# Reordering the first loads and the first attention units of an attention-plus-MLP kernel

## The chip, the cores and the metric

The kernel runs on one core of a Trainium2 chip. Its engines have in-order instruction queues and meet through semaphores: TensorE (matmuls and transposes, into PSUM), VectorE, ScalarE (activations and copies), GpSimd (here it issues nearly all loads, and makes some copies and masks), and SyncE (it issues stores and transposing DMAs). The metric is device time in microseconds of one launch. The kernel before takes 286.05 us in the median of three runs (285.69 to 287.41).

## What is computed

The inputs are q, k and v of shape (8, 8, 576, 64): batch, heads, sequence, head size. Attention goes over a window of 32 positions to either side; its result, reshaped to 4608 tokens of 512 features, goes through a two-layer network with weights w_in (512 x 2048) and w_out (2048 x 512):

```python
scores = scale * np.matmul(q, k.transpose(0, 1, 3, 2))
mask = np.abs(pos[:, None] - pos[None, :]) <= window
attn = np.exp(scores) / sum                  # after the mask, max subtracted
x = (attn @ v).transpose(0, 2, 1, 3).reshape(4608, 512)
h = x @ w_in
out = (h * sigmoid(1.702 * h)) @ w_out
```

## The kernel before

The 4608 tokens are 36 units of 128 queries; four units make a tile of 512 tokens. Since one sequence has 576 tokens, unit 4 is the first that straddles two sequences. For one unit, `scores(u)` (L248) makes the scores of eight heads in two PSUM banks and ScalarE's exponentials of them; `band(u)` (L268) multiplies by the mask on VectorE; `values(u)` (L276) multiplies by the values on TensorE, with a column of ones that gives the sum; `norm(u)` (L294) divides on VectorE. Each unit needs the values of its own 128 keys (`ve`) and the same values shifted by 64 (`vo`), which `odd_v(u)` (L208) copies in two halves: half 1 from unit u, half 0 from unit u + 1. `x_T` and `x_T2` (L308, L323) transpose one or two units of the attention's result for layer 1.

Layer 1 of tile 0 runs in 16 blocks, `layer1_plain(0, d, half, tag)` (L388): eight matmuls of 256 columns for 256 hidden features (d) and half of the tile's tokens, into the PSUM bank `tag`, then the activation on ScalarE (L400). Later tiles use a scheme with seven products in place of eight (`l1_group`, L417), which needs sums of the weights (`w1_sums`, L337). Layer 2 of tile 0 is a list of 64 matmuls of 512 columns (`layer2_plain`, L474), from which `do(self.l2, n)` takes the next n; the first 8 need the first quarter of w_out, the next 8 the second, and so on.

PSUM banks have names: t (two banks), A, C, B, E, LA, LB. A new use of a bank waits until its last reader is done. `keep_busy(n, tag, cols)` (L563) issues n dummy matmuls into a bank.

The order of the work is the order in which it is written: each engine's queue takes its instructions in program order. The opening (`opening`, L572 to L712) is written out by hand, and brings the kernel from the first loads to the start of tile 1's layer 1. It transposes the queries and keys of units 0 to 3 by TensorE in two parts (`load_first` L137, `T_first` L157), and those of tile 1 in one (`load_four` L173, `T_four` L181). Loads of one kind: `load_w1(c)` (L113) brings the c-th quarter of w_in, `load_w2(c)` (L118) that of w_out, `load_v(u)` (L194) the values of one unit, in two DMAs if the unit straddles two sequences, `load_v_part(lo, n)` (L201) those of n tokens. All of these are issued by GpSimd, between its other work: the mask (`setup_mask` L99; `cut_mask` L108, which clears the corners for units that straddle sequences) and some of the `odd_v` copies.

```python
for b, rows, cols in ((0, hi, slice(0, 32)), (0, lo, slice(32, 64)), (2, lo, slice(0, 32)), (2, hi, slice(32, 64))):
    self.nc.gpsimd.memset(self.mask[rows, b, cols], 0.0)
```

`band` reads blocks 1 and 3 of the mask for a unit inside one sequence, and block 0 or 2 for one that straddles two.

## Time and profile before

| | us |
|---|---|
| median of three runs | 286.05 |
| the profiled execution | 285.67 |
| its span | 284.0 |
| TensorE busy | 275.8 (97%) |
| VectorE busy | 215.7 (76%) |
| ScalarE busy | 193.6 (68%) |
| GpSimd busy | 131.3 (46%) |
| end of the opening on TensorE | 46.2 |

All places in time are microseconds from the start of the span. PE is TensorE's matmuls, PEld its weight loads, DVE VectorE, ACT ScalarE, POOL GpSimd, SP SyncE. A row of a timeline gives start, length, engine, line, operation, what is written and read, and in square brackets the idle time before it with what ended that time. A row of DMA issues gives the count, the size at the destination and the time from issue to landing. A line L70 is the helper through which all matmuls go, and L67 that of copies, so names of tiles tell them apart: h is layer 1, o layer 2, sc scores, pv values, tp transposes, kq and kst, qst keys and queries.

### The profile page before, as it was taken

The page shows a single profiled execution, that of the slowest core. Times are in us where ns is not written, and L with a number is a line of the kernel's source. Part 1 is how long each engine was busy: PE and PEld are TensorE (multiplying, and loading weights), DVE is VectorE, ACT ScalarE, POOL GpSimd, SP SyncE. Part 2 cuts the span into 40 slices and gives each one's busy share as a digit, 9 for nine tenths or more (in the row PEclk, how much of TensorE's full clock was granted, in tenths as well). Part 3 has the DMA queues.
Part 4 walks back from the last instruction along what each step waited for, and adds up shares of the span by engine and source line. Part 5 has one row for each costly group of instructions (what it writes and reads, how often), then busy time and mean ns, then how long its engine had stood idle before and what let it go on. Part 6 is the DMA issues. An engine that isn't in the chain of part 4 may idle for free.

```text
span 284.0 us, 9223 instructions
## 1 busy us (share of the span) xinstructions
PE 275.8 (97%) x3819; PEld 229.7 (81%) x3819; DVE 215.7 (76%) x496; ACT 193.6 (68%) x340; POOL 131.3 (46%) x199
## 2 busy tenths in 40 slices
PE   7999999999999999999999999999999999999994
PEld 7677857776777888888888788888888888888883
DVE  1758796897988888797878787888788878945631
ACT  2556775889797769667966796588758775567410
POOL 8967487896699871847084809331110000000000
PEclk9999999999999999999999999999999999999999
DMA  8999999999999999999999999994423031201033
GB/s 93 188 193 198 185 202 158 197 134 141 181 142 164 182 126 203 136 180 149 172 128 189 120 180 112 188 119 107 132 56 96 2 111 21 76 0 74 2 112 115
DMA packets 147003, 37.38 MB, mean 132 GB/s; under 512 B 133904, under 2 KB 142608, under 8 KB 146960
## 3 DMA queue, kind: packets, MB, share of 16 engines
q0 software_dynamic: 104480, 18.42, 95.5%
q1 hardware_dynamic: 42032, 17.84, 32.3%
q8 instruction: 30, 0.49, 0.7%
q10 hardware_dynamic: 448, 0.52, 0.6%
q14 instruction: 13, 0.11, 0.1%
HBM read 36.83 MB, written 9.44 MB: 163 GB/s over the span
## 4 chain that ended last, share of the span: by engine, by line
PE 80%; DMA 8%; POOL 4%; ACT 2%; DVE 2%; issue 1%; POOLq 0%
PE o L70 37%; PE h L70 36%; DMA w<-in_moe_w_out_dram 4%; DMA o_sb<-in_k_dram 4%; PE pv L70 3%; PE sc L70 2%; POOL ve L199 2%; ACT p L266 1%; POOL kq L143 1%; PE tp L332 1%; POOL w L115 1%; PE tp L242 1%; DVE x L304 1%; ACT g L429 1%; DVE h L442 0%
## 5 line engine op out<-in xcount | busy, mean ns | idle before, releaser
L429 ACT ACTIVATE g<-h 128x512 f16<-128x512 f32 x128 | 72.2, 598 | 36.1 <-PE h L70 35.9
L70 PEld LDWEIGHTS <-g 128*128 128x128 f16 x576 | 54.4, 98 | 9.7
L70 PEld LDWEIGHTS <-a 128*128 128x128 f16 x512 | 49.2, 97 | 11.4 <-issue 1.2
L70 PE MATMUL h<-xs,a 128*128 128x256 f16 x384 | 57.6, 273 | 0.4 <-DVE h L442 0.2
L70 PE MATMUL o<-w,g 128*128 128x256 f16 (+1 forms) x320 | 55.3, 295 | 0.1
L70 PEld LDWEIGHTS <-w 128*128 128x128 f16 x512 | 48.8, 98 | 7.0 <-DMA w<-in_moe_w_in_dram 0.3
L70 PE MATMUL h<-xT,w 128*128 128x256 f16 x384 | 54.1, 273 | 0.2 <-DMA w<-in_moe_w_in_dram 0.2
L199 POOL DMA_DIRECT2D ve<-in_v_dram x39 | 33.3, 859 | 36.3 <-issue 34.2
L70 PEld LDWEIGHTS <-gs 128*128 128x128 f16 x384 | 36.7, 98 | 5.2 <-issue 0.4
L266 ACT ACTIVATE p<-sc 128x512 bf16<-128x512 f32 x72 | 36.6, 621 | 3.3 <-PE sc L70 3.3
L70 PE MATMUL o<-b,gs 128*128 128x256 f16 x256 | 37.7, 273 | 0.5 <-ACT o L67 0.5
L70 PE MATMUL o<-b,g 128*128 128x256 f16 x256 | 37.3, 273 | 0.0
L442 DVE TENSOR_TENSOR h<-h,s 128x512 f32<-128x512 f32 x32 | 22.3, 698 | 18.9 <-PE h L70 18.9
L67 ACT COPY h<-h 128x512 f32<-128x512 f32 x32 | 18.9, 589 | 15.9 <-PE h L70 15.5
L304 DVE TENSOR_TENSOR x<-pv,rec 128x256 f16<-128x256 f32 (+1 forms) x53 | 27.6, 520 | 1.8
L131 POOL DMA_DIRECT2D kst<-in_k_dram x31 | 26.5, 856 | 5.3 <-DMA w<-in_moe_w_out_dram 2.2
L131 POOL DMA_DIRECT2D qst<-in_q_dram x35 | 28.0, 804 | 1.8 <-DMA qT<-qst 1.2
L274 DVE TENSOR_TENSOR p<-p,mask 128x1024 bf16<-128x1024 bf16 x36 | 24.8, 691 | 4.9 <-ACT p L266 4.3
L218 POOL COPY vo<-ve 64x264 int32<-64x264 int32 x31 | 15.5, 500 | 26.2 <-PE pv L70 24.8
L448 DVE TENSOR_TENSOR h<-h,s 128x512 f32<-128x512 f32 x32 | 22.4, 699 | 4.7 <-PE h L70 4.2
L67 ACT COPY s<-h 128x512 f32<-128x512 f32 x32 | 19.2, 601 | 1.3
L70 PE MATMUL h<-xs,w 128*128 128x256 f16 x128 | 19.2, 273 | 0.0
(86 smaller groups left out, 367.9 us busy)
## 6 DMA issues: line engine op xcount, KB each, us to landing
out_dram<-o_sb SPq DMA_DIRECT2D x33, 256.0 KB, 3.2
ve<-in_v_dram POOLq DMA_DIRECT2D x31, 128.0 KB, 6.0
kst<-in_k_dram POOLq DMA_DIRECT2D x25, 128.0 KB, 6.4
qst<-in_q_dram POOLq DMA_DIRECT2D x21, 128.0 KB, 6.0
w<-in_moe_w_in_dram POOLq DMA_DIRECT2D x4, 512.0 KB, 8.7
w<-in_moe_w_out_dram POOLq DMA_DIRECT2D x4, 512.0 KB, 11.9
qst<-in_q_dram POOLq DMA_DIRECT2D x7, 96.0 KB, 5.4
ve<-in_v_dram POOLq DMA_DIRECT2D x10, 64.0 KB, 7.8
```

Of the source, the lines that this page charges most:

```text
L67: (eng.copy if eng is self.nc.scalar else eng.tensor_copy)(out, in_)
L70: self.nc.tensor.matmul(out, lhsT, rhs, start=start, stop=stop, skip_group_check=True)
L115: self.nc.gpsimd.dma_start(self.w1[:, :, c * 512:c * 512 + w], self.w_in[:, c * 512:c * 512 + w].rearrange("(k p) f -> p k f", p=128))
L131: self.nc.gpsimd.dma_start(t[off:off + n], src[b, :, s:s + n, :].rearrange("h s d -> s h d"))
L199: self.nc.gpsimd.dma_start(t[off:off + n, :, :self.D], self.v[b, :, s:s + n, :].rearrange("h s d -> s h d"))
L218: eng.tensor_copy(words(vo[64:128]), words(self.ve[u % 9][64:128]))
L266: self.nc.scalar.activation(p[:, eo].rearrange("k h s -> k (h s)"), sc[eo], AF.Exp, scale=self.scale)
L274: (eng or self.nc.vector).tensor_mul(pv, pv, msk.to_broadcast([128, 8, 2, SQ]))
L304: dve.tensor_mul(x[:, 4 * at:4 * (at + n), :].rearrange("p (b h) d -> p b h d", b=n), acc[:, :, :, :D], r.to_broadcast([128, n, 4, D]))
L429: act.activation(g[:, f, 256 * half:256 * half + 256], bank.rearrange("p (i n) -> p i n", i=2), AF.Gelu_apprx_sigmoid)
L442: dve.tensor_add(e, b, s7)
L448: dve.tensor_add(c, b, s7)
```

## The change

Only `opening` changes. Among the loads, the second keys and queries of units 0 to 3 go ahead of the first quarter of w_in; the values of unit 3 and the first half of unit 4's go ahead of its second quarter, and the other half behind its fourth; `odd_v(3)` on GpSimd moves up behind tile 1's keys; `cut_mask` moves down to where `odd_v(6)` is issued, which on GpSimd's queue is behind the keys of unit 8. The memset of `idle` is cut into eight.

Units 2 and 3 are then transposed and scored directly behind units 0 and 1, with other banks and copying engines; the layer-1 blocks of tile 0 follow in the order (half 0: d 0 to 3), (half 1: 0 to 3), (half 0: 4, 5), (half 1: 4, 5), (half 0: 6, 7), (half 1: 6, 7), where before it was half 0: 0 to 5, half 1: 0 to 5, half 0: 6, 7, half 1: 6, 7. From unit 4 on, the layer-2 matmuls stand in other places, 20 of them instead of 24 within the opening; those left over run later, at the next `do(self.l2)` without a count (L819).

```diff
-        dve.memset(self.idle, 0.0)
+        for i in range(8):
+            dve.memset(self.idle[:, 64 * i:64 * i + 64], 0.0)
...
         for u in (0, 1, 2):
             self.load_v(u)
+        self.load_first("k", 1)
+        self.load_first("q", 1)
         self.load_w1(0)
         self.setup_mask()
-        self.load_first("k", 1)
-        self.load_first("q", 1)
-        self.cut_mask()
+        self.load_v(3)
+        self.load_v_part(512, 64)
         self.load_w1(1)
-        self.load_v(3)
-        self.load_v(4)
         self.load_w1(2)
         self.load_four("k")
+        self.odd_v(3, pool)
         self.load_four("q")
         self.load_w1(3)
-        self.odd_v(3, pool)
+        self.load_v_part(576, 64)
...
         self.norm(0)
         self.norm(1)
-        self.keep_busy(2, "E")
-        self.x_T(0, "LA", act)
-        self.keep_busy(4, "E")
-        self.x_T(1, "LB", act)
-        self.T_first("k", 1, "AC", (dve, dve))
...
-        self.layer1_plain(0, 0, 0, "B", gelus)
-        self.T_first("q", 1, ("LA", "LB"), (dve, act))
-        self.layer1_plain(0, 1, 0, "E", gelus)
-        h[:] = ["B", "E", "LB", "LA", "B", "E", "LB", "LA"]
+        self.T_first("k", 1, "BE", (act, act))
+        self.T_first("q", 1, ("LA", "LB"), (act, dve))
+        self.x_T(0, "B", dve)
+        self.x_T(1, "E", dve)
         self.odd_v(2, dve, (1,))
+        self.keep_busy(3, "LA")
         self.scores(2, "t")
         self.scores(3, "AC")
-        self.layer1_plain(0, 2, 0, "LA", gelus)
-        self.layer1_plain(0, 3, 0, "LB", gelus)
-        self.do(gelus)
...
+        l1(0, 0, "B")
+        l1(0, 1, "E")
         self.band(2)
         self.odd_v(2, dve, (0,))
         self.band(3)
-        self.keep_busy(4, "t")
         self.values(2, "t")
         self.norm(2)
-        self.keep_busy(4, "A")
+        self.keep_busy(3, "LA")
         self.values(3, "AC")
         self.norm(3)
-        l1(0, 4)
+        self.keep_busy(8, "LA")
+        l1(0, 2, "LA")
         self.x_T2(2, "A", dve)
-        l1(0, 5)
+        l1(0, 3, "LB")
...
         for i in (3, 1, 2):
             self.w1_sums((i,), 0)
+        self.cut_mask()
         for u in (6, 7):
             self.odd_v(u, pool)
...
-        l1(1, 0, 1)
+        l1(1, 0, "B")
+        l1(1, 1, "E")
+        l1(1, 2, "LA")
+        l1(1, 3, "LB")
         self.T_four("k", "AC", (dve, dve))
...
-        l1(1, 2, 3)
+        l1(0, 4, "B")
+        l1(0, 5, "E")
         self.T_four("q", "AC", (dve, act))
-        l1(1, 4, 5)
+        l1(1, 4, "LB")
+        l1(1, 5, "LA")
+        for i in (3, 1):
+            self.w1_sums((i,), 1)
         self.odd_v(4, dve)
+        self.odd_v(5, dve, (1,))
         self.scores(4, "t")
         self.scores(5, "AC")
-        for i in (3, 1):
-            self.w1_sums((i,), 1)
         for d, tag in ((6, "B"), (7, "E")):
             self.layer1_plain(0, d, 0, tag, gelus)
-        self.do(self.l2, 3)
         self.scores(6, "t")
-        self.do(self.l2, 3)
+        self.do(self.l2, 4)
         self.scores(7, "AC")
         self.do(gelus)
-        self.do(self.l2, 2)
+        self.do(self.l2, 4)
         self.band(4)
-        self.odd_v(5, dve)
         self.band(5)
         self.band(6)
+        self.odd_v(5, dve, (0,))
         self.values(4, "t")
...
         self.band(7)
-        self.do(self.l2, 4)
         self.values(6, "t")
         self.norm(6)
-        self.do(self.l2, 4)
+        l1(1, 6, "B")
         self.values(7, "AC")
         self.norm(7)
-        l1(1, 6, 7)
+        l1(1, 7, "E")
+        self.do(self.l2, 4)
         self.x_T2(4, "A", act)
         self.do(self.l2, 4)
         self.x_T2(6, "t", dve)
         self.do(self.l2, 4)
```

More of the change, by code (lines that the diff above doesn't have):

```diff
@@ L627, in opening, with l1 @@
         self.norm(1)
-        self.keep_busy(2, "E")
-        self.x_T(0, "LA", act)
-        self.keep_busy(4, "E")
-        self.x_T(1, "LB", act)
-        self.T_first("k", 1, "AC", (dve, dve))
-        h, n, gelus = [], [0], []
-        def l1(half, *ds):
-            for d in ds:
-                self.layer1_plain(0, d, half, h[n[0] % len(h)])
-                n[0] += 1
-        self.layer1_plain(0, 0, 0, "B", gelus)
-        self.T_first("q", 1, ("LA", "LB"), (dve, act))
-        self.layer1_plain(0, 1, 0, "E", gelus)
-        h[:] = ["B", "E", "LB", "LA", "B", "E", "LB", "LA"]
+        self.T_first("k", 1, "BE", (act, act))
+        self.T_first("q", 1, ("LA", "LB"), (act, dve))
+        self.x_T(0, "B", dve)
+        self.x_T(1, "E", dve)
         self.odd_v(2, dve, (1,))
+        self.keep_busy(3, "LA")
         self.scores(2, "t")
         self.scores(3, "AC")
-        self.layer1_plain(0, 2, 0, "LA", gelus)
-        self.layer1_plain(0, 3, 0, "LB", gelus)
-        self.do(gelus)
+        gelus = []
+        def l1(half, d, tag):
+            self.layer1_plain(0, d, half, tag)
+        l1(0, 0, "B")
+        l1(0, 1, "E")
         self.band(2)
@@ L699, in opening @@
         self.band(7)
-        self.do(self.l2, 4)
         self.values(6, "t")
         self.norm(6)
-        self.do(self.l2, 4)
+        l1(1, 6, "B")
         self.values(7, "AC")
         self.norm(7)
-        h[:] = "BE"
-        n[0] = 0
-        l1(1, 6, 7)
+        l1(1, 7, "E")
+        self.do(self.l2, 4)
         self.x_T2(4, "A", act)
```

## The prediction

> **What bounds the kernel now.** I read the page first (engine shares, the chain that ended last), then the chain in order of time, then each engine's timeline over the first 90 us, then the landing times of single DMAs.

> ```profile
> span 284.0 us, 9223 instructions
> PE 80%; DMA 8%; POOL 4%; ACT 2%; DVE 2%; issue 1%; POOLq 0%
> ```

> TensorE holds 80% of the chain. The profiled run took 285.67 us, so 1.67 us lie around the span of 284.0; the median of the three runs, 286.05, is 0.38 above that run, and I add my difference to the median.

> ```profile
> 88.00:284.00 196.00, 191.76 (x2443) 165.62 (x2441) 150.88 (x350) 131.66 (x235) 61.33 (x94) 1.00 1.10 116
> 46.23:66.00 19.77, 19.75 (x168) 14.71 (x167) 17.52 (x34) 15.76 (x30) 18.71 (x27) 1.00 2.03 163
> ```

> In this view by windows (length, then busy time of PE, PE's weight loads, DVE, ACT, POOL, then the granted clock) TensorE is busy for 19.75 of the 19.77 us behind the opening, which ends at 46.23. Nothing after it is edited. So the change is worth what it takes off the opening, less what it pushes out of it: four layer-2 matmuls, since the opening issues 20 of them instead of 24.

> ```profile
> 14.11 11.40 DMA o_sb<-in_k_dram
> 25.51 0.28 issue
> 25.80 0.68 POOL ve L205
> 26.48 12.65 DMA w<-in_moe_w_out_dram
> 39.13 0.04 issue
> 39.17 1.02 PE o L70 x4
> ```

> The chain (start, length, what) runs up to 39.17 through GpSimd's issues and two landings: the load of w_out's second quarter waits at L205 until an earlier DMA has landed, and TensorE then waits for that quarter. The opening is bound by the order of loads; TensorE follows closely behind.

> **The waits on GpSimd's queue.**

> ```profile
> 18.74 0.79 POOL L115 DMA_DIRECT2D w<-in_moe_w_in_dram  x1 [1.57 <-DMA w<-in_moe_w_in_dram]
> 29.29 0.70 POOL L205 DMA_DIRECT2D ve<-in_v_dram  x1 [2.05 <-DMA o_sb<-in_q_dram]
> 34.29 0.89 POOL L131 DMA_DIRECT2D kst<-in_k_dram  x1 [1.68 <-DMA w<-in_moe_w_out_dram]
> ```

> Counting GpSimd's DMAs in program order, the 17th (18.74) waits for the 9th, the 24th for the 16th, and the 27th, the keys of unit 8, for the 19th: w_out's first quarter. So one DMA may be issued when the eighth before it has landed. After the change the 27th and the 19th are the same two.

> ```profile
> w<-in_moe_w_out_dram POOLq DMA_DIRECT2D x1, 512.0 KB, 11.6
> 22.44 0.76 POOL L119 DMA_DIRECT2D w<-in_moe_w_out_dram  x1
> ```

> That quarter lands at 22.44 + 11.6 = 34.0. The same loads stand ahead of it before and after, only in another order, and the queues are full all the while, so I keep 34.0.

> **The change part by part.**

> ```profile
> 0.94 0.27 DVE L576 MEMSET idle<- 128x256 uint32 x1 [0.94 <-PEq L915]
> ```

> Memset of idle: one instruction becomes eight of an eighth each, off the path, since the first transposes wait for keys to land. Cost 0; bounds 0 and, if each of the eight still takes 0.07, 0.3.

> Second keys and queries ahead of w_in's first quarter, values 3 and half of 4 ahead of the second:

> ```profile
> kq<-in_k_dram POOLq DMA_DIRECT2D x1, 256.0 KB, 6.2
> 8.45 0.70 POOL L143 DMA_DIRECT2D kq<-in_k_dram  x1
> w<-in_moe_w_in_dram POOLq DMA_DIRECT2D x1, 512.0 KB, 7.8
> 5.99 0.78 POOL L115 DMA_DIRECT2D w<-in_moe_w_in_dram  x1
> ```

> The second keys land at 8.45 + 6.2 = 14.65, w_in's first quarter at 5.99 + 7.8 = 13.8. With the second queries (256 KB, landing near 15.9) these are 1024 KB, which move from about 9.9, when values 2 land, to 15.9: 170 KB per us. In the new order (keys, queries, quarter) I estimate keys at 11.4, queries at 12.9, the quarter at 15.9. Units 2 and 3 can thus be transposed from 12.6, behind the values of units 0 and 1. What is late next are w_in's second quarter (about 19.8) and, behind it, the keys of tile 1:

> ```profile
> 26.88 1.11 PE L189 MATMUL tp<-ident,o_sb 128*64 128x128 bf16 x32
> ```

> Both orders have eight layer-1 blocks ahead of this line. In the new one six blocks and one pair of x transposes follow w_in's second quarter. From the rows below a block is 0.88 and the pair 0.44: With TensorE at that point at 20.1 (the landing and the end of the dummy matmuls) 20.1 + 5.7 = 25.8, against 26.88, and the keys land at 14.11 + 11.40 = 25.5 now and slightly sooner then. Gain here 1.1, bounds 0.6 and 1.4.

> That gain is not kept, I think, because of **cut_mask**. It was done at 10.4 and held up unit 0's masking by half a microsecond:

> ```profile
> 9.32 2.06 ACT L266 ACTIVATE p<-sc 128x512 bf16<-128x512 f32 x4 [0.42 <-PE sc L70]
> 10.51 0.69 DVE L274 TENSOR_TENSOR p<-p,mask 128x1024 bf16<-128x1024 bf16 x1 [0.56 <-POOL mask L111]
> 9.81 0.60 POOL L111 MEMSET mask<- 64x32 bf16 x4
> 35.87 0.91 DVE L274 TENSOR_TENSOR p<-p,mask 128x1024 bf16<-128x1024 bf16 x1 [1.95 <-ACT p L266]
> 34.69 4.03 ACT L266 ACTIVATE p<-sc 128x512 bf16<-128x512 f32 x8
> ```

> Unit 0's two exponentials, half of the four from 9.32, end only at 10.4 too, so its removal gives at most 0.1. In its new place it sits on GpSimd's queue behind the keys of unit 8, which are issued from 34.29 to 35.18. Four memsets of 0.60 end at 35.8, and unit 4, which straddles two batches, is the first whose mask reads the blocks they write. So band(4) cannot start before 35.85: the very time at which it starts now, 35.87, when exponentials held it. The eight exponentials from 34.69 should start near 33.5, since TensorE's 1.1 carries through the layer-1 blocks to the table load ahead of them; unit 4's two would then end at 34.5. The new wait stands where they stood. Queued behind it on VectorE are bands 5 and 6, half of odd_v(5), and the norms of units 4 and 5.

> ```profile
> 36.82 0.39 DVE L218 COPY vo<-ve 64x264 int32<-64x264 int32 x1
> 38.79 0.19 DVE L303 RECIPROCAL rec<-pv 128x8 f32<-128x8 f32 x1
> 40.72 0.68 DVE L274 TENSOR_TENSOR p<-p,mask 128x1024 bf16<-128x1024 bf16 x1
> 41.85 1.92 PE L70 MATMUL h<-xT,w 128*128 128x256 f16 x16
> 43.61 0.61 PE L332 MATMUL tp<-identh,x 128*128 128x128 f16 x8
> 44.05 1.03 PE L70 MATMUL o<-w,g 128*128 128x512 f16 x4
> 44.92 0.61 PE L332 MATMUL tp<-identh,x 128*128 128x128 f16 x8
> ```

> Of this run of VectorE one instruction leaves, the first half of odd_v(5): 36.82 to 37.24, 0.42. The rest keeps its order, so unit 7's band ends at 41.0 instead of 41.4, and values(7) ends at 41.4 instead of 41.85. From there TensorE has before: two layer-1 blocks (41.85 to 43.61), a pair of x transposes (0.44), four layer-2 matmuls (0.87), the same pair and four again: 1.76 + 2 x 0.44 + 2 x 0.87 = 4.38, to 46.23. After: one block, three fours, two pairs: 0.88 + 2.61 + 0.88 = 4.37, to 45.8. **Opening: -0.4**, and four layer-2 matmuls left over. Bounds: -1.0 if band(4) didn't bind, +0.8 below.

> On TensorE the new order then has idle time, some 2.5 us by my estimate: at scores(6), from 33.8 to the end of unit 4's exponentials, at values(5), about 1.0 until odd_v(5)'s half is done near 38.4, and 0.5 each at values(6) and values(7), for norm 4 and band 7. Layer-2 matmuls stood there as cover, but those of w_out's second quarter cannot run before 39.13.

> The leftover four, 0.87 by the rows at 44.05 and 44.92, run at the end of tile 0's first half:

> ```profile
> 68.47 1.90 PE L70 MATMUL o<-w,g 128*128 128x512 f16 x8
> 72.56 0.22 PE L70 MATMUL pv<-ve,p 128*64 128x65 bf16 x1
> 73.36 0.20 DVE L303 RECIPROCAL rec<-pv 128x8 f32<-128x8 f32 x1
> 73.72 1.03 PE L70 MATMUL o<-b,gs 128*128 128x256 f16 x8 [0.46 <-ACT o L67]
> ```

> TensorE waits 0.46 at 73.72 for ScalarE, so the four are about half hidden there. But values(8), which start at 72.56 and end near 72.9, would end at 72.9 - 0.4 + 0.9 = 73.4, and unit 8's norm on VectorE, which leads the work up to 81 us, would start near 73.5 instead of 73.36. So the 0.4 is spent: **+0.1 in all** (bounds -0.4, if the four are wholly hidden, and +0.5, if not at all). 286.05 + 0.1 = 286.1.

> GpSimd's odd_v(3) ahead of the queries of tile 1 blocks the queue until values 3 and half of 4 land (about 17.4): the queries are issued near 19 instead of 16. Three loads wait in the DMA queues then, so it costs nothing; without that cover it would be up to 3.

> [...] Band(4) takes 0.91 at 35.87 and 0.69 at 10.51; at 35.84 to 37.5 GpSimd copies for odd_v:

> ```profile
> 35.84 0.40 POOL L220 COPY vo<-ve 64x264 int32<-64x264 int32 x1 [0.22 <-DMA ve<-in_v_dram]
> 36.30 0.76 POOL L218 COPY vo<-ve 64x264 int32<-64x264 int32 x1
> 37.11 0.40 POOL L220 COPY vo<-ve 64x264 int32<-64x264 int32 x1
> ```

> A GpSimd copy takes 0.40 or 0.76, a VectorE band 0.69 or 0.91: they hold each other up. [...]

> **The rivals.**

> 1. *Band(4) doesn't wait, or the four hide.* If the memsets come earlier than I have them, exponentials bind: the opening ends 1.0 earlier, and the later stage gives half back: 286.05 - 1.0 + 0.5 = 285.5; with the four hidden too, 285.0. For: exponentials really come 1.2 earlier. Against: the wait at 34.29 is on a landing that the change doesn't move.
> 2. *TensorE takes all that the loads allow.* Start of tile 1's keys at 25.1 instead of 26.88 and nothing given back: 286.05 - 1.8 = 284.3. Against: ScalarE's exponentials and w_out's landing.
> 3. *Slower: cut_mask late, and a collision.* The price is a later band(4) on VectorE. Three copies of 0.40, each pushing one instruction of that run, are 1.2, without my 0.4 gain of the opening: 286.05 + 1.2 - 0.4 + 0.5 = 287.3. It decides once band(4) starts after 36.3 or the run from it to unit 4's norm takes more than 2.9 (35.87 to 38.79 now). Each microsecond by which w_out's first quarter lands later goes the same way in full.
> 4. *The loads don't land earlier* (the second keys still near 14). Then the tile's keys are taken near 26.9 again, which the wait of band(4) hides: 286.1.

> **How the numbers follow.** Forecast with rival 4: 0.56. Rival 1: 0.20; rival 2: 0.05; rival 3: 0.19, with 0.06 of it beyond 1%. The range reaches over rivals 1 and 3, 285.0 to 287.3, and the runs before spread by 1.7 us, so 284.9 to 287.4. One per cent is 2.9 us, about what a measurement of this kernel tells from no change: faster by more 0.03 (rival 2 and something besides), slower by more 0.06.

> **What would show it.** Right: transposes of the second keys near 12.7 and of tile 1's near 25.8; band(4) released by GpSimd's mask near 35.9, not by an exponential; the opening's last four layer-2 matmuls starting near 44.9; twelve layer-2 matmuls ahead of unit 10's scores near 70. Wrong: band(4) near 34.6 (rival 1), or from 36.5 on (rival 3); queries of tile 1 late at their transposes; or stalls behind 81 us, of which I expect none.

## The result, and the profile after

The changed kernel is slower: 287.73 us in the median (287.45 to 289.93) against 286.41 for the kernel before in the same comparison, a ratio of 1.0059 with a 95% interval of 1.0035 to 1.0084. The forecast was 286.1 with a range up to 287.4, so the median lies just outside it. Measured a second time the ratio was 1.0069 (1.0037 to 1.0100).

The page of the changed kernel, its first lines (span, then busy time, share and count of each engine):

```profile
span 287.8 us, 9233 instructions
PE 276.4 (96%) x3819; PEld 230.6 (80%) x3819; DVE 215.4 (75%) x503; ACT 194.1 (67%) x340; POOL 130.2 (45%) x199
```

TensorE has the same 3819 matmuls and 0.6 us more busy time, but the span is 3.8 us longer than before (287.8 against 284.0). This execution took 289.47 us. The time is spent in one place. TensorE's timeline of the changed kernel (start, length, line, operation, written and read tiles, count, idle time before and what ended it):

```profile
12.63 1.55 PE L168 MATMUL tp<-ident,kq 64*64 64x64 bf16 x64
...
15.17 0.63 PE L70 MATMUL sc<-kq 64*64 64x64 bf16 x39
18.24 0.42 PE L70 MATMUL sc<-kq 64*64 64x64 bf16 x9 [2.45 <-issue]
18.60 3.21 PE L70 MATMUL h<-xT,w 128*128 128x256 f16 x16
...
29.89 1.11 PE L189 MATMUL tp<-ident,o_sb 128*64 128x128 bf16 x32
...
49.42 0.60 PE L70 MATMUL h<-xT,w 128*128 128x256 f16 x4
```

The second keys are transposed at 12.63, as forecast. The 48 score matmuls of units 2 and 3 start at 15.17, and after the 39th TensorE stands still for 2.45 us. The releaser is "issue": nothing in the trace that an engine or a DMA does ends this wait, and it falls in the middle of one unit's scores, with nothing new to wait for. Behind it the 16 matmuls of layer 1 take 3.21 us; the same row of the kernel before takes 1.92 (at 41.85). Tile 1's keys come at 29.89 (26.88 before, 25.8 forecast), and the opening ends at 49.42 (46.23 before, 45.8 forecast). The view by windows shows why the 16 take longer (columns as in the prediction; the granted clock is the third from the end):

```profile
15.00:18.00 3.00, 0.79 (x42) 0.52 (x39) 1.97 (x5) 1.08 (x2) 0.76 (x1) 0.98 1.55 195
18.00:20.40 2.40, 2.16 (x18) 1.60 (x19) 0.65 (x1) 1.75 (x3) 2.18 (x4) 0.50 1.25 208
20.40:23.00 2.60, 2.60 (x45) 1.79 (x44) 0.78 (x3) 1.81 (x3) 2.60 (x4) 0.83 1.39 200
```

Behind the idle time TensorE's clock is granted by half (0.50 from 18.00 to 20.40). So two things are paid: 2.45 us of standing still and 3.21 - 1.92 = 1.29 us of half clock. Opening: 49.42 - 46.23 = 3.19 us later; the remaining 3.8 - 3.19 = 0.6 comes behind it, where twelve layer-2 matmuls now stand in place of eight:

```profile
71.57 2.76 PE L70 MATMUL o<-w,g 128*128 128x512 f16 x12
```

The half clock is not in every execution. The mean granted clock of the whole execution is 0.994 or less in ten of 21 executions of the changed kernel, which take 288.7 to 291.3 us, and 0.998 or more in the other eleven, which take 286.9 to 288.1. The profile of the second comparison is one of the latter:

```profile
15.51 0.62 PE L70 MATMUL sc<-kq 64*64 64x64 bf16 x39
17.92 0.31 PE L70 MATMUL sc<-kq 64*64 64x64 bf16 x9 [1.78 <-issue]
18.16 1.92 PE L70 MATMUL h<-xT,w 128*128 128x256 f16 x16
...
28.17 1.11 PE L189 MATMUL tp<-ident,o_sb 128*64 128x128 bf16 x32
...
47.70 0.60 PE L70 MATMUL h<-xT,w 128*128 128x256 f16 x4
```

The same gap behind the same 39th matmul, 1.78 us here, then layer 1 at its usual 1.92. The opening ends at 47.70 and the span is 286.1.

### The profile page after: what moved, and what is told of

The parts are those of the page before. It is cut to its first block, busy times and chain, and to the rows that moved or that the text cites. A ratio compares the mean times of both kernels' runs of the same rounds, so it can differ in the third digit from the quotient of the medians.

```text
span 287.8 us, 9233 instructions
## 1 busy us (share of the span) xinstructions
PE 276.4 (96%) x3819; PEld 230.6 (80%) x3819; DVE 215.4 (75%) x503; ACT 194.1 (67%) x340; POOL 130.2 (45%) x199
## 4 chain that ended last, share of the span: by engine, by line
PE 83%; DVE 6%; ACT 3%; DMA 2%; issue 2%; POOL 2%; DVEq 0%; POOLq 0%
PE o L70 37%; PE h L70 36%; PE pv L70 4%; PE sc L70 3%; DMA kq<-in_q_dram 2%; DVE kq L67 1%; DVE b L356 1%; PE tp L332 1%; ACT p L266 1%; POOL ve L199 1%; DVE h L442 1%; DVE x L304 1%; PE junk L70 1%; POOL kq L143 1%; ACT g L429 1%
## 5 line engine op out<-in xcount | busy, mean ns | idle before, releaser
L429 ACT ACTIVATE g<-h 128x512 f16<-128x512 f32 x128 | 72.1, 598 | 35.9 <-PE h L70 35.6
L70 PEld LDWEIGHTS <-g 128*128 128x128 f16 x576 | 54.6, 98 | 9.9
L70 PEld LDWEIGHTS <-a 128*128 128x128 f16 x512 | 49.3, 97 | 10.9 <-issue 0.7
L70 PE MATMUL h<-xs,a 128*128 128x256 f16 x384 | 57.6, 272 | 0.2
L70 PEld LDWEIGHTS <-w 128*128 128x128 f16 x512 | 49.7, 99 | 7.8 <-issue 0.5
L70 PE MATMUL h<-xT,w 128*128 128x256 f16 x384 | 55.1, 278 | 0.3 <-ACT g L400 0.3
L70 PE MATMUL o<-w,g 128*128 128x256 f16 (+1 forms) x320 | 55.0, 294 | 0.0
L199 POOL DMA_DIRECT2D ve<-in_v_dram x37 | 31.9, 864 | 31.9 <-issue 27.0
L70 PEld LDWEIGHTS <-gs 128*128 128x128 f16 x384 | 36.7, 98 | 4.8
L266 ACT ACTIVATE p<-sc 128x512 bf16<-128x512 f32 x72 | 36.7, 617 | 5.5 <-PE sc L70 5.4
L70 PE MATMUL o<-b,gs 128*128 128x256 f16 x256 | 37.7, 273 | 0.0
L70 PE MATMUL o<-b,g 128*128 128x256 f16 x256 | 37.3, 273 | 0.0
L442 DVE TENSOR_TENSOR h<-h,s 128x512 f32<-128x512 f32 x32 | 22.3, 698 | 17.6 <-PE h L70 17.5
L131 POOL DMA_DIRECT2D kst<-in_k_dram x31 | 26.5, 856 | 11.3 <-PE tp L242 3.5
L67 ACT COPY h<-h 128x512 f32<-128x512 f32 x32 | 18.8, 588 | 16.1 <-PE h L70 15.6
L131 POOL DMA_DIRECT2D qst<-in_q_dram x35 | 28.0, 804 | 3.1 <-DMA kst<-in_k_dram 3.1
L274 DVE TENSOR_TENSOR p<-p,mask 128x1024 bf16<-128x1024 bf16 x36 | 24.6, 686 | 5.7 <-ACT p L266 5.7
L218 POOL COPY vo<-ve 64x264 int32<-64x264 int32 x31 | 15.0, 484 | 30.2 <-PE pv L70 25.9
L67 ACT COPY s<-h 128x512 f32<-128x512 f32 x32 | 19.2, 601 | 1.2
L70 PE MATMUL h<-xs,w 128*128 128x256 f16 x128 | 19.2, 273 | 0.0
## 6 DMA issues: line engine op xcount, KB each, us to landing
out_dram<-o_sb SPq DMA_DIRECT2D x33, 256.0 KB, 3.1
w<-in_moe_w_in_dram POOLq DMA_DIRECT2D x4, 512.0 KB, 9.4
w<-in_moe_w_out_dram POOLq DMA_DIRECT2D x4, 512.0 KB, 11.3
```

The source lines that it names most:

```text
L67: (eng.copy if eng is self.nc.scalar else eng.tensor_copy)(out, in_)
L70: self.nc.tensor.matmul(out, lhsT, rhs, start=start, stop=stop, skip_group_check=True)
L131: self.nc.gpsimd.dma_start(t[off:off + n], src[b, :, s:s + n, :].rearrange("h s d -> s h d"))
L199: self.nc.gpsimd.dma_start(t[off:off + n, :, :self.D], self.v[b, :, s:s + n, :].rearrange("h s d -> s h d"))
L218: eng.tensor_copy(words(vo[64:128]), words(self.ve[u % 9][64:128]))
L266: self.nc.scalar.activation(p[:, eo].rearrange("k h s -> k (h s)"), sc[eo], AF.Exp, scale=self.scale)
```

## What the gap is: the program's blocks

Two rows of the changed kernel's DMA view speak of a queue that no load of the kernel uses: the whole span, and the quarter of a microsecond from 15.75 (packets, MB, share).

```profile
q8 instruction: 30, 0.49, 0.7%
q8 instruction: 1, 0.02, 24.7%
```

Thirty transfers of 0.49 MB in all are 16 KB each. TensorE has 3819 matmuls and as many weight loads, 7638 instructions, which is 255 to a transfer. So I read q8 as TensorE's program, and count 256 instructions, that is 128 matmuls, to a block; in e1 below 127 matmuls lie between two gaps. One such block is transferred in the window at 15.75; in the trace its packet starts at 15.88, and 2.4 us later the gap ends. In every profile with a gap in the opening (this kernel's two and those of seven kernels below) it ends 2.3 to 2.5 us after such a start.

Counting TensorE's matmuls from the start, the gap stands exactly behind the 351st. The previous boundary, behind matmul 351 - 128 = 223, was crossed at 12.5. That gave the theory of the **program's supply** (of the fetch of instructions, in some of the expectations): when TensorE crosses into a block, the block after it begins to be fetched and is there 5 to 6 us later; a TensorE that has done its next 128 matmuls sooner than that waits. In the new order the transposes of units 2 and 3 and the scores lie close together: 128 matmuls from 12.5 to 15.8. In the old order two layer-1 blocks and dummy matmuls lie between them, and the 351st matmul comes at 18.1, the 352nd at 18.2. The trace of the kernel before has the block's packet at 15.81, and 2.4 us behind it is 18.2 as well: it had no time to spare at this boundary, although its profile shows no gap there.

## The experiments

The rivals to the supply theory (F in the expectations) were that the new order of work waits for a copy, a bank or a load that the profile doesn't name (R), that the load order itself costs the time (L: queues, landings), that the moved `cut_mask` does, or the four layer-2 matmuls. The comparisons were made on several chips, each kernel beside runs of the kernel before on the same chip. Where nothing else is said, ratios are to that.

**Fewer matmuls ahead of the gap.** Dummy matmuls are merged into wider ones, so that the block boundary falls at a later place of the work. Two degrees of it in the changed kernel:

```diff
 # e1: 56 matmuls fewer               # e2: 30 fewer
-keep_busy(60, "E", 96)              -keep_busy(60, "E", 96)
+keep_busy(14, "E", 384)             +keep_busy(30, "E", 160)
-keep_busy(6, "E")
+keep_busy(3, "E", 512)
-keep_busy(4, "E")
+keep_busy(2, "E", 512)
-keep_busy(10, "E")
+keep_busy(5, "E", 512)
```

> The kernel after, with the 80 dummy matmuls of the first 10 us merged into 24 wider ones of about the same length: 56 matmuls (112 TensorE instructions) fewer ahead of the scores of units 2 and 3. Theory F (instruction fetch: TensorE's program comes in blocks of 256 instructions over the same DMA engines as the loads, and a block asked for in the opening takes some 6 us): the gap of 2.45 us within scores(3) is gone or under 0.5 us and lies elsewhere, the granted clock stays at 1.00, and the time is 1.3 to 2 us under that of the kernel after: 285.5 to 286.4. Theory R (the new order itself: scores(3) waits for a copy, bank or load that the profile does not name): the gap of about 2.4 us stays within scores(3), and the time stays at 287.5 or above.

> The kernel after, with the first 60 dummy matmuls (96 columns) as 30 of 160 columns: 30 matmuls (60 instructions) fewer. Theory F: the block boundary moves 30 matmuls on, from the scores of unit 3 into values(2) behind the first two layer-1 blocks; the gap is there, and about 0.5 to 1.2 us instead of 2.45; time 286.2 to 287.2. Theory R: the gap stays within scores(3), with 2.4 us, and the time at 287.5 or above.

Rows of TensorE's timeline, the first two of e1, the third of e2:

```profile
14.14 0.57 PE L168 MATMUL tp<-ident,kq 64*64 64x64 bf16 x22 [0.29 <-issue]
20.26 0.22 PE L70 MATMUL pv<-vo,p 128*64 128x65 bf16 x1 [0.78 <-issue]
```

```profile
19.66 0.19 PE L70 MATMUL pv<-ve,p 128*64 128x65 bf16 x1 [1.18 <-issue]
```

The gap left the scores and went where the count puts it: in e1 behind the 223rd matmul, in the middle of transposes, and at the 351st, in the values of unit 3; in e2 at the 351st, in the values of unit 2. A wait for the data of unit 3's scores would have stayed with those scores. Both stayed slower than before, 1.0050 (1.0035 to 1.0065) and 1.0087 (1.0065 to 1.0110): the gap was moved, and in e1 split, not removed. For e1 I had expected at most 0.5 and 285.5 to 286.4 us (0.29 + 0.78 and 287.38 came). For e2 I had expected the gap within 0.5 to 1.2 (1.18 came) but a time up to 287.2 (288.11 came).

**The same in the kernel before**, where no gap stood: once with e1's merged dummies, once with 40 tiny dummy matmuls added ahead of the transposes of the second keys.

```diff
 # e4
+for _ in range(40):
+    self.mm(junk[0:64, 0:16], self.idle[0:64, 0:64], self.idle[0:64, 0:16], start=True, stop=True)
 self.T_first("k", 1, "AC", (dve, dve))
```

> The kernel before, with the same 80 dummy matmuls merged into 24. A control: the kernel before shows no gap of this kind, so Theory F expects no change (within 0.4 us of before), and so does R. If it gains 1 us or more, the dummies themselves cost time and the first run tells nothing of fetches.

> The kernel before, with 40 tiny dummy matmuls (64x64, 16 columns) ahead of the transposes of the second keys, where TensorE waits for that load anyway. Theory F: the block boundary comes 40 matmuls earlier, into the transposes of the second queries near 16.5 us, and TensorE stands there until about 18.2: a gap of 1.2 to 1.8 us, and the time rises by 1 to 2 us. Theory R: no gap, and the time rises by 0.4 us at most (the part of the tiny matmuls that the wait does not cover).

Neither showed a gap in the opening: 1.0027 (1.0007 to 1.0048) and 1.0022 (1.0003 to 1.0041). For e4 that is a miss of mine, not a verdict: 37 of the tiny matmuls took 1.33 us, so the stretch from the 223rd to the 351st still took 5.2 us (13.2 to 18.4), and the block had time to come. In e3 the opening ended at 46.25, as before, and yet its span was 1.2 longer. Of that, 0.9 is a gap, also put down to "issue", far from the opening; another kernel (e7, below) shows one too. TensorE's timelines of e3 and of e7:

```profile
164.78 0.49 PE L70 MATMUL o<-b,gs 128*128 128x256 f16 x3 [0.88 <-issue]
```

```profile
83.50 0.60 PE L70 MATMUL h<-xT,w 128*128 128x256 f16 x4 [0.87 <-issue]
```

Counted in the stream these stand 11 and 7 matmuls ahead of a multiple of 128 from the opening's boundaries, the later one by more; that TensorE's other instructions, which I didn't count, shift the boundary so is a guess. In e7 a block's packet starts at 81.08, 2.4 us before the gap ends, as in the opening; in e3 the last one starts at 161.05, 3.7 us before, so that a late block is not shown there. No other profile, the kernel before's among them, has such a gap. A block seems to come late now and then in a dense stage too, and about 0.9 us of difference between single executions can come from such gaps. Whether it makes the spread of the kernel before (285.5 to 288.8) was not tried.

**Still fewer dummies, and the two other suspects.** e5 makes 67 matmuls fewer than the changed kernel. e6 is e5 with `cut_mask` issued behind the load of tile 1's keys instead of behind the keys of unit 8. e7 is e6 with four of the left-over layer-2 matmuls back in the opening.

```diff
 # e5
-keep_busy(60, "E", 96)
+keep_busy(10, "E", 512)
 # and the smaller groups of 6, 4, 10, 5 and 3 dummies cut to 2, 1, 4, 2 and 2, most of them of 512 columns
 # e6, besides
 self.load_four("k")
+self.cut_mask()
 self.odd_v(3, pool)
...
-self.cut_mask()
 # e7, besides
 self.band(7)
+self.do(self.l2, 4)
 self.values(6, "t")
```

> The kernel after, with its 88 dummy matmuls up to the scores of units 2 and 3 as 21 of 512 or 256 columns, of about the same length: 67 matmuls fewer. Theory F, counted in blocks: boundaries lie behind the 223rd and the 351st matmul of the stream, and a block comes about 6 us after the boundary before it was crossed; with 67 fewer, the 351st falls at the end of the eight dummies behind values(3), near 19.7, and the gap shrinks to 0.3 us or less. Keys of tile 1 are then transposed near 25.8 to 26.3 and the opening ends at 45.6 to 46.1, as predicted for the change itself; time 286.0 to 286.6, that is 0.3 us or less from before. Theory R (the order itself, apart from fetches, is slower): 287.2 or above.

> As e5_few, and cut_mask issued behind tile 1's keys, where GpSimd waits for values 3 anyway, instead of behind the keys of unit 8. If cut_mask holds band(4) once fetches don't (my prediction's step): band(4) starts 0.5 to 1.2 us earlier than in e5_few, near 34.8, and the opening ends 0.3 to 0.9 earlier. If ScalarE's exponentials hold it: no change against e5_few (within 0.2 us).

> As e6_few_cut, with four more layer-2 matmuls of the opening between band(7) and values(6), as in the kernel before (24 in all). TensorE waits there for norm 4 and the activation table, so they should cost 0 to 0.3 us of the opening and take 0.4 to 0.9 off the stage at 68 to 74 us: 285.2 to 285.9, faster than before by up to 0.3%. If the leftover four matmuls were hidden in the later stage already, the time is that of e6_few_cut.

TensorE's timeline of e5:

```profile
14.65 0.44 PE L168 MATMUL tp<-ident,kq 64*64 64x64 bf16 x12 [1.34 <-issue]
```

I had not counted the earlier boundary. The gap now stands behind the 223rd matmul, inside the transposes of the second queries: with fewer matmuls ahead, the 95th (the boundary before) was done only at 8.75, and the block came 5.9 us later. The three were alike: 1.0037 (1.0015 to 1.0059), 1.0036 (1.0013 to 1.0059), 1.0047 (1.0022 to 1.0071), with the opening's end at 47.54, 47.56 and 47.57. So with the gap in place `cut_mask` costs nothing, and four more layer-2 matmuls inside the opening cost it nothing either: they fill idle time. e5 and e7 missed my times (up to 286.6 and up to 285.9; 287.83 and 288.35 came): in the profiles of all three the half clock followed this gap too, and the four matmuls in e7 brought no gain that shows.

**The loads alone.** The work of the kernel before with the order of loads of the changed one (`cut_mask` and half of unit 4's values placed to fit):

```diff
 # in the kernel before
+load_first("k", 1); load_first("q", 1)
 load_w1(0)
 setup_mask()
-load_first("k", 1); load_first("q", 1)
-cut_mask()
+load_v(3); load_v_part(512, 64)
 load_w1(1)
-load_v(3); load_v(4)
 load_w1(2)
 load_four("k")
+cut_mask(); odd_v(3, pool)
 load_four("q")
 load_w1(3)
-odd_v(3, pool)
+load_v_part(576, 64)
```

> The kernel before with the new order of loads alone (cut_mask behind tile 1's keys; TensorE's and VectorE's order unchanged). Theory F: the loads cost nothing by themselves; TensorE's block boundary lies where it lay before, and w_in's first quarter, about 2 us later, delays the first layer-1 block by 0.6 us or less: 285.9 to 286.9, no gap of over 1 us. A rival by which the new order of loads is what slows the kernel (L: transfers or queue waits): 287.2 or above.

Ratio 1.0003 (0.9977 to 1.0029). TensorE's timeline:

```profile
15.93 1.05 PE L70 MATMUL h<-xT,w 128*128 128x256 f16 x8 [0.77 <-DMA w<-in_moe_w_in_dram]
19.73 1.92 PE L70 MATMUL h<-xT,w 128*128 128x256 f16 x16 [0.51 <-DMA w<-in_moe_w_in_dram]
```

With the old work the later quarters of w_in are waited for, 0.77 and 0.51, and the opening ends at 46.91; in the time that is not to be seen. No gap of the "issue" kind. So the loads alone are not the cause, as far as the interval goes (it reaches to +0.8 us); it takes the new order of TensorE's work.

**What the block waits for.** In e9 the whole queue of GpSimd is held back by `odd_v(3)`, moved ahead of w_in's second and third quarters and tile 1's keys, so that fewer loads should be in flight when the block is fetched.

```diff
+self.odd_v(3, pool)
 self.load_w1(1)
 self.load_w1(2)
 self.load_four("k")
-self.odd_v(3, pool)
```

> The kernel after with GpSimd's odd_v(3), which waits for values 3 and half of 4, ahead of the loads of w_in's second and third quarter and of tile 1's keys: these loads are issued near 18 instead of 11.4 to 13.8, so far fewer bytes stand in the queues when the block is asked for at 12.3. If the block waits behind queued loads: its transfer comes before 15.0 (15.75 in the kernel after) and the gap in scores(3) ends before 17.5 instead of 18.2. If a block takes its 6 us whatever is queued: as in the kernel after, within 0.3 us. The time itself rises by some microseconds, since the loads are late.

TensorE's timeline and two rows by windows (the last two numbers are the DMA share and GB/s):

```profile
17.96 0.31 PE L70 MATMUL sc<-kq 64*64 64x64 bf16 x9 [2.15 <-issue]
```

```profile
13.00:15.00 2.00, 1.75 (x66) 1.55 (x58) 1.66 (x7) 1.56 (x3) 0.00 (x0) 1.00 1.47 192
15.00:18.00 3.00, 0.84 (x46) 0.56 (x46) 2.12 (x6) 1.08 (x2) 0.79 (x2) 1.00 0.76 55
```

The gap ended at 17.96 (18.24 and 17.92 in the two profiles of the changed kernel). That looks like an answer, but it is none: the block was asked for near 12.5 and its packet started at 15.52, and until then the loads issued earlier still moved as much as in the changed kernel (192 GB/s from 13 to 15, against 191). The thin stretch, 55 GB/s against 195, came almost wholly after the transfer. The next block tells more. Its boundary was crossed at 17.96, when nothing was being moved (0 GB/s from 17.5 to 19.5, a row is shown in the last section), and its packet started at 19.95, 2.0 us later; in the two profiles of the changed kernel, with 200 GB/s around it, that took 4.0 and 3.9. So queued loads may well be part of what makes a block late. It is one case, and in e10 below the first block's packet started 1.4 us after its crossing with 183 GB/s moving (6.03 to 7.40), so the question stays open. The kernel took 292.48 in its one execution, with the half clock and with its later loads late.

**More matmuls ahead.** In the opposite direction, 92 dummies of 64 columns instead of 60 of 96: 32 more matmuls in about the same time, so that the boundaries are crossed earlier. e11 is e10 with the early `cut_mask` of e6, e12 is e11 with the four layer-2 matmuls of e7.

```diff
-keep_busy(60, "E", 96)
+keep_busy(92, "E", 64)
```

> The kernel after with MORE instructions: the first 60 dummy matmuls of 96 columns as 92 of 64 (about the same length, ended before the first keys land). Theory F: all block boundaries move 32 matmuls earlier in the work; the one that fell into scores(3) at 15.8 falls into scores(2) near 15.3, and the one before it into the ten dummies near 9.4 instead of 12.3, so the block is asked for 2.8 us earlier and is there near 15.4. Gap 0.4 us or less, granted clock 1.00, keys of tile 1 transposed at 25.8 to 26.3, opening ended at 45.5 to 46.1, and 286.0 to 286.8. If the wish for fewer instructions were the point, or the order itself were slow, it stays at 287.4 or above.

> As e10_more, with cut_mask issued behind tile 1's keys, where GpSimd waits for values 3. Without the fetch gap the exponentials of unit 4 should end near 34.6; if cut_mask, ended near 35.9, then holds band(4) in e10_more, band(4) starts 0.5 to 1.2 us earlier here and the opening ends 0.3 to 0.9 earlier; if not, within 0.2 us of e10_more.

> As e11_more_cut, with four more layer-2 matmuls in the opening between band(7) and values(6), 24 in all as before the change. If the leftover four cost about 0.5 us later on: 285.4 to 286.1, faster than before by 0.1 to 0.3%. If they were hidden: as e11_more_cut.

No gap in any of the three, and the time of the kernel before: 1.0002 (0.9981 to 1.0024), 1.0029 (0.9999 to 1.0058), 1.0000 (0.9973 to 1.0027). They are not clean, though, and missed my forecasts (up to 286.8 for e10, up to 286.1 for e12; 287.23 and 286.99 came). The first program block is now transferred at 7.4 instead of 9.2, and in all three the first values land later. The DMA view of e10 up to 20 us, and VectorE's timeline of e10:

```profile
ve<-in_v_dram POOLq DMA_DIRECT2D x4, 128.0 KB, 7.0
```

```profile
10.82 0.29 DVE L220 COPY vo<-ve 64x264 int32<-64x264 int32 x1 [1.77 <-DMA ve<-in_v_dram]
```

The median from issue to landing is 7.0 us, against 4.9 in the changed kernel; VectorE waits 1.77 us for the values, and unit 0's values on TensorE start at 12.4 instead of 11.2. That the earlier block delays those loads is argued from the coincidence alone. In e10 the mask does release the band of unit 4, in e11 an exponential. VectorE's timelines of e10 and of e11:

```profile
36.57 0.69 DVE L274 TENSOR_TENSOR p<-p,mask 128x1024 bf16<-128x1024 bf16 x1 [1.57 <-POOL mask L111]
```

```profile
36.21 0.72 DVE L274 TENSOR_TENSOR p<-p,mask 128x1024 bf16<-128x1024 bf16 x1 [1.80 <-ACT p L266]
```

The band starts 0.36 sooner in e11, and the opening ends at 46.77 instead of 47.07. That is not the mask's doing, though: e11 is 0.32 ahead already when tile 1's keys are transposed (27.23 against 27.55), and e12, with `cut_mask` early too, has the keys at 27.51, the band at 36.49 and the end at 47.04. From the keys to the band it is 9.02 us with `cut_mask` late and 8.98 in both with it early: it costs the band 0.04, and the end of the opening nothing.

**Long matmuls ahead of the boundary.** This test keeps the count of matmuls up to the boundary: the first two layer-1 blocks, 16 matmuls of 256 columns, go ahead of the scores of unit 3, so that the 351st matmul is the 15th of layer 1. e14 adds the early `cut_mask` and the four layer-2 matmuls. e15 is the changed kernel again, on the same chip.

```diff
 self.scores(2, "t")
-self.scores(3, "AC")
 gelus = []
+self.layer1_plain(0, 0, 0, "B", gelus)
+self.layer1_plain(0, 1, 0, "E", gelus)
+self.scores(3, "AC")
+self.do(gelus)
...
-l1(0, 0, "B")
-l1(0, 1, "E")
...
-self.keep_busy(3, "LA")
+self.keep_busy(6, "LA")
+l1(0, 2, "LA")
 self.values(3, "AC")
 self.norm(3)
-self.keep_busy(8, "LA")
-l1(0, 2, "LA")
-self.x_T2(2, "A", dve)
 l1(0, 3, "LB")
+self.keep_busy(3, "t")
+self.x_T2(2, "A", dve)
```

> Both layer-1 blocks of the first pair (16 matmuls of 256 columns) go ahead of the scores of unit 3; the count of instructions stays. Theory of the program block (TensorE's next 256 instructions come about 6 us after the last boundary was crossed, whatever they are): the 351st matmul is now the 15th of layer 1 instead of the 39th of scores; it is issued near 17.8, the next comes at 18.2 to 18.3, so the stall falls from 2.45 to 0.3 to 0.6 us and stands inside or behind layer 1. Tile 1's keys are then transposed near 26.2 (27.9 to 29.9 in the changed kernel); the time is 1.5 to 2.5 us below the changed kernel's on this chip, within 0.5 us of the kernel before or faster than it. Rival, that something in the scores themselves or a wait on a buffer stalls TensorE: the gap stays 2 us or more, in front of the same scores of unit 3, or goes to none; time as the changed kernel's.

> As the run with layer 1 ahead of scores 3, with cut_mask behind tile 1's keys and four more layer-2 matmuls between band 7 and values 6 (24 in the opening, as in the kernel before). Theory of the program block: opening ends near 45.7 (46.23 before), nothing is left over for later, time 0.3 to 0.8 us below the kernel before. Rival, that the opening's end is held by exponentials and bands whatever TensorE does earlier: opening ends at 46.2 or later, time as before.

> The changed kernel again, on the chip of these runs. Theory: the gap stands behind the 351st matmul, 2.3 to 2.6 us; where the clock stays at 1.00 behind it, layer 1 takes 1.9 and tile 1's keys are transposed near 27.9, time 1.0 to 1.6 us above the kernel before; where the clock falls to half, as in the first profile, keys near 29.9 and 3 us above. Rival, that the first profile was an odd execution: no gap.

TensorE's timeline of e13:

```profile
16.02 1.81 PE L70 MATMUL h<-xT,w 128*128 128x256 f16 x15
18.16 0.28 PE L70 MATMUL h<-xT,w 128*128 128x256 f16 x1 [0.34 <-issue]
18.38 0.45 PE L70 MATMUL sc<-kq 64*64 64x64 bf16 x24
...
23.98 3.67 PE L70 MATMUL h<-xT,w 128*128 128x256 f16 x32 [0.79 <-DVE xT L67]
27.57 1.11 PE L189 MATMUL tp<-ident,o_sb 128*64 128x128 bf16 x32
```

The gap is 0.34, between the 15th and the 16th matmul of layer 1, as the theory had said; the next block comes at 18.16, where it came before. In e14 layer 1 starts 0.24 later and there is no gap at all. The half clock is gone too: the twelve executions of e13 have a clock of 0.997 or more. On this chip the changed kernel is at 1.0069 and e13 at 1.0025 of the kernel before: 0.44%, or 1.3 us, between them. That is the price of the gap with its clock, less what e13's own order costs. Against the kernel before, e13 is 1.0025 (1.0003 to 1.0046) and e14 1.0024 (1.0002 to 1.0046). The rest of what I expected failed: tile 1's keys come at 27.57 instead of 26.2, since my order then waits 0.79 for a copy of x on VectorE, and the openings end at 47.11 and 47.17, not 45.7. No version here beats the kernel before.

## Why the prediction was wrong, point by point

**The loads land about as forecast: right.** Second keys: issued at 5.99, 6.2 to landing, 12.2 (forecast 11.4, so 0.8 late); they and the queries were transposed from 12.63 (12.6). Rows of the changed kernel's GpSimd timeline and DMA view, with w_out's first quarter behind them:

```profile
5.99 0.72 POOL L143 DMA_DIRECT2D kq<-in_k_dram  x1
kq<-in_k_dram POOLq DMA_DIRECT2D x1, 256.0 KB, 6.2
22.49 0.79 POOL L119 DMA_DIRECT2D w<-in_moe_w_out_dram  x1
w<-in_moe_w_out_dram POOLq DMA_DIRECT2D x1, 512.0 KB, 11.8
```

w_out's first quarter lands at 34.3 (34.0). Tile 1's queries, held behind `odd_v(3)`, are issued at 18.6 (19) without harm. In e8 the order of loads by itself cost nothing measurable.

**"What is late next": this step failed.** I named w_in's second quarter and tile 1's keys as what comes next, and let TensorE go through transposes, x and scores at the rate of their rows. Its own program was not on the list, and the clock neither. From 15.8 to 18.2 it stood still, by the supply theory for want of instructions: 1.78 and 2.45 us in the two profiles, plus 1.29 of half clock in one. Take both off the 29.89 at which tile 1's keys are transposed and 26.15 is left, near my 25.8; the 28.17 of the other profile less 1.78 gives 26.4, with its unit 0 values 0.35 later. So by subtraction a gain of 0.5 to 0.7 is left of my 1.1, and the stall took back more than twice that. It is an estimate that no run shows: in e10 to e14, with no gap or one of 0.34, tile 1's keys came at 27.23 to 27.63, later than the 26.88 of the kernel before. There the first values were late (e10 to e12) or the order had a wait of its own (0.79 in e13 and e14). My bounds for this step, 0.6 to 1.4 of gain, had no case in which TensorE is short of instructions; no rival had it.

**cut_mask holds band(4): not seen.** Everything ahead of the band was late. VectorE's and GpSimd's timelines of the changed kernel:

```profile
38.87 0.69 DVE L274 TENSOR_TENSOR p<-p,mask 128x1024 bf16<-128x1024 bf16 x1 [1.65 <-ACT p L266]
35.55 0.51 POOL L111 MEMSET mask<- 64x32 bf16 x4
```

The mask is done at 36.06 (forecast 35.8), and an exponential releases the band at 38.87. Without the gap (e10) the mask does release it, but only 0.04 later than exponentials would, as worked out above. How long it would hold a band that is ready near 35, as I had forecast, no run shows.

**The opening's end.** From tile 1's keys to the end of the opening the new order takes 19.53 us in both profiles (29.89 to 49.42, 28.17 to 47.70), and 19.52 to 19.54 in all the other versions of it but e9, with `cut_mask` late or early and with 20 or 24 layer-2 matmuls; I had 20.0. The old order takes 19.35 (26.88 to 46.23), and 19.19 to 19.32 in e3, e4 and e8. So behind tile 1's keys the new order gains nothing. The 0.4 that I took off VectorE's run, for half an odd_v(5), was not seen: from band(4) to the end of the opening it is 10.36 before, 10.55 and 10.56 in the changed kernel and 10.50 to 10.56 in e10 to e12. In e10 bands 5 and 6 wait 0.17 and 0.29 for exponentials, so a copy less on VectorE saves nothing there. From keys at 26.15 the opening would end at 45.7, if nothing else held it. That this is near my 45.8 is partly luck: the gain in it is that of the keys, which I had let cut_mask take back, and not the 0.4 on VectorE. Of the 2.5 us idle time that I listed behind 33 us, the second profile shows 1.6: 0.59 at scores(6), 0.77 at the values, 0.25 at a layer-1 block.

**The left-over four: right in direction, the size is uncertain.** What the span has grown by beyond the opening is 3.8 - 3.19 = 0.6 in the first profile and 2.1 - 1.47 = 0.6 in the second, against my 0.5 (from -0.4 to +0.1). But putting them back into the opening takes only 0.2 off the rest of the span in e12 (against e11) and in e14 (against e13), and the times don't tell these kernels apart. Inside the opening they are free: 19.53 and 19.54 us from tile 1's keys with them.

**VectorE's bands beside GpSimd's copies** were no part of the loss, since the band and GpSimd's copies lay apart. In e13 they meet: two bands take 1.73 us together and two copies 0.76 and 0.75, where a band alone takes 0.69 and a copy 0.40; yet the opening ends no later behind tile 1's keys (19.54). The two bands together take 0.35 longer there; that a copy pushes an instruction of VectorE by its full 0.40, as the third rival's 1.2 has it, no run shows.

**The rivals.** The result lies near the third rival (287.3) by its size, but not by its mechanism: no late band, no collision. The kernels without the gap lie at 1.0000 to 1.0029, and my sum of +0.1 us is 1.0003. But they carry other small delays, and none has the early keys of the forecast, so they neither prove the sum nor refute it.

## What to carry to other kernels

Ahead of moving short matmuls together, count them: in this opening, with 190 to 200 GB/s of loads moving, TensorE got 128 matmuls (256 instructions) per 4.8 to 6.6 us. From that I estimate that here a stretch of matmuls under about 40 to 50 ns each (4.8 to 6.6 us over 128), longer than one block, runs dry, even when its data are there. A wait put down to "issue" on TensorE in the middle of like instructions, at the same count in every profile (2.45 and 1.78 us behind the 351st), is the sign; long matmuls put ahead of the boundary hid it (0.34 us left in e13, none in e14), and merging dummy matmuls only moved it (0.29 + 0.78 in e1, 1.18 in e2, 1.34 in e5). Such a gap can also cost the clock (1.29 us in the first profile), and then shows as two groups of execution times (286.9 to 288.1 and 288.7 to 291.3 us here).

## What the runs showed of the hardware

**Supply.** From the crossing of one boundary to the first instruction behind the next: 5.8 and 5.1 us in the changed kernel, 5.4 in e13, 5.5 in e9, 5.9 in e5, 4.8 and 6.4 in e1, 6.6 in e2. By the packets' starts in the traces the block's transfer on q8 begins 2.5 to 4.2 us after the crossing, and its instructions run 2.3 to 2.5 us after that. What fills the first part, and why it varies, stays open; it was 2.0 for the one block of e9 that was asked for with no load moving.

**The clock.** Behind stalls of 1.3 to 2.5 us it fell to half in five profiles (the first of the changed kernel, e5, e6, e7 and e9), but not behind the 1.78 us of the changed kernel's second. Windows of half a microsecond, of the changed kernel, then of e9, then of e5, each where the half clock begins and where it ends:

```profile
17.50:18.00 0.50, 0.00 (x0) 0.00 (x0) 0.39 (x1) 0.00 (x0) 0.24 (x1) 0.85 1.23 205
...
21.00:21.50 0.50, 0.50 (x5) 0.40 (x4) 0.00 (x0) 0.49 (x2) 0.50 (x1) 0.73 1.43 200
```

```profile
18.50:19.00 0.50, 0.50 (x6) 0.42 (x5) 0.00 (x0) 0.50 (x2) 0.50 (x2) 0.93 0.00 0
...
22.00:22.50 0.50, 0.50 (x9) 0.10 (x8) 0.50 (x1) 0.00 (x0) 0.50 (x2) 0.66 1.19 199
```

```profile
16.00:16.50 0.50, 0.50 (x48) 0.50 (x34) 0.48 (x2) 0.17 (x1) 0.00 (x0) 0.55 1.30 202
...
19.00:19.50 0.50, 0.50 (x4) 0.38 (x3) 0.13 (x1) 0.50 (x1) 0.50 (x1) 0.53 1.22 201
```
